# A new order of steps for the first batch of an attention and GELU kernel: squares and scalings moved between ScalarE, VectorE and GpSimd

## The chip, the cores and the metric

The kernel runs on one core of a Trainium2 chip. The metric is device time in microseconds (us), the median of several runs. Engines are named as the profile names them: PE is TensorE (PEld its weight loads), DVE VectorE, ACT ScalarE, POOL GpSimd, SP SyncE.

## What is computed

Cosine attention over 8 batches, 12 heads, 448 positions and a head size of 64, then two matrix products with an exact GELU between them, all inputs and the output in float32:

```python
q_n = q / (np.linalg.norm(q, axis=-1, keepdims=True) + 1e-06)
k_n = k / (np.linalg.norm(k, axis=-1, keepdims=True) + 1e-06)
scores = np.matmul(q_n, k_n.transpose(0, 1, 3, 2)) / tau
attn = softmax(scores, axis=-1)
x = np.matmul(attn, v)            # then to [3584, 768]
h = x @ w_in                      # w_in is [768, 2048]
g = 0.5 * h * (1.0 + erf(h / sqrt(2)))
out = g @ w_out                   # w_out is [2048, 768]
```

## The kernel before

The twelve heads of a batch are three quads of four heads. Quads are numbered through all batches, so quads 0, 1 and 2 are the first batch and quad 3 is the first of the second. A quad's q and k lie in one tile, two pairs of heads `s` side by side and the two heads of a pair on the two halves of the 128 partitions. Positions are in seven chunks `c` of 64. The normalisation works on *units*: unit 0 is pair s = 0 of quad 0, unit 1 is pair s = 1 of quad 0, and from there a unit is a whole quad (unit 2 is quad 1, unit 3 is quad 2, unit 4 is quad 3). What a unit goes through, by function and line:

- `load_qk` (L129, SP queue; the first half of k by ACT's): q and k to SBUF, in one of four buffers. `load_v` (L141), `load_wi` (L381) and `load_wo` (L388) are issued by GpSimd's queue and change the type to bf16 on the way; a `load_wi` or `load_wo` index stands for a part of the weight.
- `square(u, parts)` (L154 on ACT, L156 on GpSimd or DVE): squares of q (`Q`) or k (`K`). `reduce` (L165, DVE): their sums over the head size. `logs` (L172) and `roots` (L178 or L181), both on ACT: the root as exp(0.5 ln). `inverses` (L188 or L190, then L192): adds 1e-6 and takes the reciprocal rn, on DVE for the first batch. `scale(u, ((engine, i),))` (L208): multiplies q (i = 0) or k (i = 1) by rn into bf16; the result is the tile `qkb`.
- `transposes(u, i)` (L225, PE, seven small matmuls into a PSUM bank) and `copies(u, i)` (L230, DVE) give `qkT`. From the second batch on, a DMA transposes instead.

A quad's attention: `scores(g, ((s, c), (s, c)))` (L246, PE) gives two banks, `exps` (L253, ACT) turns both into bf16, 128x896 in one instruction; seven of these make a quad. Scores alternate between two pairs of PSUM banks, so each waits for the exps two before it. `sums` (L266) adds the rows by a matmul with ones; `turned`, `inverted` and `spread` (L297, L314, L318, DVE) make the reciprocal sums; `values` (L289, PE) multiplies with v; `normalise` (L323, DVE, one input in PSUM) writes x. A batch's x then goes through `first` (L642 `hp`, PE, and L678, the GELU on ACT) and `second_pieces` (L352 `op`, PE). `hp` of a block needs x of quads 0 and 1 first (kd 0 to 3), of quad 2 last (kd 4 and 5).

PSUM tiles for transposes and half of the values take two banks in turn. `spin(n)` (L403) issues n matmuls whose result nobody reads, into the bank that comes next in that turn; it waits for that bank to be free as the others do.

The order is set by hand: the schedule is manual, so each engine runs its instructions in the order in which the program lists them, and waits only for data and buffers. For the first batch that list is written out in `attention_first`, one call per step. For later batches `attention`, `group` and `both` set it. Before `attention_first` stand the loads, 20 spins, and `late`, a GpSimd copy that waits for the second half of the first k.

Of the kernel before, what the change touches and what calls it, by code (L numbers as in the profile page):

```python
# [16 lines left out]
def kernel(  # L17
# [129 lines left out]
    def square(u, parts=None):  # L147
        g, s0, s1 = units[u]
        if g not in sq_t:
            sq_t[g] = sqp.tile([128, 2, 2, C, D], F32, tag="sq", name=f"sq{g}")  # L150
        sq, t = sq_t[g][:, :, s0:s1], qk_t[g][:, :, s0:s1]
        for eng, part in parts or ((nc.gpsimd, slice(0, 2)),):
            if eng is nc.scalar:
                eng.activation(sq[:, part], t[:, part], AF.Square)  # L154
            else:
                eng.tensor_tensor(sq[:, part], t[:, part], t[:, part], ALU.mult)  # L156

    def reduce(u, part=slice(0, 2)):
        g, s0, s1 = units[u]
        sq = sq_t[g][:, :, s0:s1]  # L160
        n, j = place[u]
        if n not in nq_t:
            nq_t[n] = nrm.tile([128, len(groups[n]), 2, s1 - s0, C], F32, tag="nq", name=f"nq{n}")
        nq = nq_t[n][:, j]
        nc.vector.tensor_reduce(nq[:, part], sq[:, part], mybir.AxisListType.X, ALU.add)  # L165
# [239 lines left out]
    def attention_first():  # L405
        x_t[0] = xp.tile([128, KD, S], BF16, tag="x", name="x0")
        DV, AC, GP = nc.vector, nc.scalar, nc.gpsimd
        Q, K = slice(0, 1), slice(1, 2)
        square(0, ((AC, Q),))
        square(0, ((AC, K),))  # L410
        reduce(0, Q)
        reduce(0, K)
        square(1, ((AC, Q),))
        upto(load_v, 1)
        logs(0)
        reduce(1, Q)
        roots(0)
        square(1, ((AC, K),))
        inverses(0)
        square(2, ((AC, Q),))  # L420
        scale(0, ((DV, 1),))
        scale(0, ((GP, 0),))
        reduce(1, K)
        transposes(0, 1)
        upto(load_v, 2)
        transposes(0, 0)
        logs(1)
        copies(0, 1)
        roots(1)
        square(2, ((AC, K),))  # L430
        copies(0, 0)
        upto(load_wi, 1)
        inverses(1)
        spin(2)
        scores(0, ((0, 0), (0, 1)))
        square(3, ((AC, Q),))
        scores(0, ((0, 2), (0, 3)))
        reduce(2, K)
        scale(1, ((GP, 1),))
        exps(0, ((0, 0), (0, 1)))  # L440
        reduce(2, Q)
        scale(1, ((GP, 0),))
        upto(load_qk, 5)
        spin(4)
        transposes(1, 1)
        exps(0, ((0, 2), (0, 3)))
        copies(1, 1)
        logs(2)
        upto(load_wi, 2)
        spin(1)  # L450
        transposes(1, 0)
        roots(2)
        scores(0, ((0, 4), (0, 5)))
        square(3, ((AC, K),))
        inverses(2)
        copies(1, 0)
        scale(2, ((GP, 1),))
        exps(0, ((0, 4), (0, 5)))
        reduce(3, Q)
        spin(3)  # L460
        scores(0, ((1, 0), (1, 1)))
        scores(0, ((1, 2), (1, 3)))
        exps(0, ((1, 0), (1, 1)))
        reduce(3, K)
        scale(2, ((GP, 0),))
        upto(load_qk, 6)
        transposes(2, 1)
        exps(0, ((1, 2), (1, 3)))
        scores(0, ((1, 4), (1, 5)))
        copies(2, 1)  # L470
        logs(3)
        spin(1)
        scores(0, ((0, 6), (1, 6)))
        roots(3)
        upto(load_wi, 3)
        transposes(2, 0)
        exps(0, ((1, 4), (1, 5)))
        inverses(3)
        copies(2, 0)
        exps(0, ((0, 6), (1, 6)))  # L480
        scale(3, ((GP, 0),))
        spin(3)
        scores(1, ((0, 0), (1, 0)))
        exps(1, ((0, 0), (1, 0)))
        scores(1, ((0, 1), (1, 1)))
        sums(0, range(2))
        sums(0, range(2, 4))
        exps(1, ((0, 1), (1, 1)))
        scale(3, ((GP, 1),))
        scores(1, ((0, 2), (1, 2)))  # L490
        sums(0, range(4, 7))
        exps(1, ((0, 2), (1, 2)))
        scores(1, ((0, 3), (1, 3)))
        transposes(3, 0)
        turned(0)
        exps(1, ((0, 3), (1, 3)))
        upto(load_wi, 4)
        scores(1, ((0, 4), (1, 4)))
        values(0, range(2))
        copies(3, 0)  # L500
        exps(1, ((0, 4), (1, 4)))
        scores(1, ((0, 5), (1, 5)))
        inverted(0)
        transposes(3, 1)
        square(4, ((GP, K),))
        spread(0, 1)
        exps(1, ((0, 5), (1, 5)))
        scores(1, ((0, 6), (1, 6)))
        values(0, range(2, 4))
        copies(3, 1)  # L510
        values(0, range(4, 7))
        exps(1, ((0, 6), (1, 6)))
        spread(0, 0)
        square(4, ((GP, Q),))
        square(5)
        upto(load_wo, 2)
        upto(load_v, 3)
        scores(2, ((0, 0), (1, 0)))
        sums(1, range(2))
        normalise(0, 0)  # L520
        exps(2, ((0, 0), (1, 0)))
        scores(2, ((0, 1), (1, 1)))
        normalise(0, 1)
        sums(1, range(2, 4))
        exps(2, ((0, 1), (1, 1)))
        scores(2, ((0, 2), (1, 2)))
        reduce(4, K)
        sums(1, range(4, 7))
        exps(2, ((0, 2), (1, 2)))
        scores(2, ((0, 3), (1, 3)))  # L530
        values(1, range(2))
        turned(1)
        values(1, range(2, 4))
        exps(2, ((0, 3), (1, 3)))
        inverted(1)
        scores(2, ((0, 4), (1, 4)))
        spread(1, 0)
        sums(2, (0,))
        exps(2, ((0, 4), (1, 4)))
        sums(2, (1,))  # L540
        spread(1, 1)
        scores(2, ((0, 5), (1, 5)))
        values(1, range(4, 7))
        exps(2, ((0, 5), (1, 5)))
        scores(2, ((0, 6), (1, 6)))
        sums(2, (2,))
        normalise(1, 0)
        exps(2, ((0, 6), (1, 6)))
        sums(2, (3,))
        sums(2, (4,))  # L550
        reduce(4, Q)
        sums(2, (5,))
        values(2, (0,))
        sums(2, (6,))
        values(2, (1,))
        normalise(1, 1)
        logs(4)
        values(2, (2,))
        roots(4)
        values(2, (3,))  # L560
        turned(2)
        inverted(2)
        inverses(4)
        scale(4)
        spread(2, 1)
        values(2, (4,))
        values(2, (5,))
        values(2, (6,))
        spread(2, 0)
        normalise(2, 0)  # L570
        normalise(2, 1)
        done.update({square: 6, reduce: 5, root: 5, scale: 5, transposes: 5})

# [179 lines left out]
```

## Time and profile before

| what | us |
|---|---|
| median of 4 runs | 418.43 (417.96 to 418.74) |
| profiled execution | 417.54 |
| its span in the profile | 415.8 |
| PE busy | 409.4 (98%) |
| ACT busy | 246.3 (59%) |
| DVE busy | 188.1 (45%) |
| POOL busy | 167.2 (40%) |

The granted clock of TensorE is 1.00 over the span. The profile is one execution; its time is the span plus what lies around it, and it is compared with the median of the runs by the difference of the two. A row of a timeline gives the start in the span, the busy time, engine, line, operation, the tile written and those read with their shapes, the count of instructions in the row, and in brackets how long the engine sat idle before it and what ended that. Neighbouring instructions overlap by about 0.1 us in their busy times, so what an instruction costs in a full queue is the distance between starts. Matmul ends are modelled. In the first batch, ACT's first exp of quad 0 starts at 10.31, the first of quad 1 at 18.60 and the first of quad 2 at 24.56; the last ends at 30.68; the first `hp` matmul starts at 32.34.

### The profile page before, as it was taken

To read this page: it belongs to the slowest core of one execution; us is meant where nothing else is said; L and a number is where in the kernel's file an instruction comes from. 1 tells how busy PE (TensorE), PEld (TensorE's weight loads), DVE (VectorE), ACT (ScalarE), POOL (GpSimd) and SP (SyncE) were. 2 spreads that over 40 slices of the span, in tenths; PEclk is the share of its full clock that TensorE was granted. 3 is DMA by queue.
4 is the path that set the end of the run, shared out by engine and by line. 5 is a ranking of instruction groups with operands and counts; after the bars stand their busy time and mean duration, and the time that the engine had idled before them with its cause. 6 is when DMAs were issued, how large, how long until landed. Compare 5 with 4: busy or idle time off the path is not lost.

```text
span 415.8 us, 8254 instructions
## 1 busy us (share of the span) xinstructions
PE 409.4 (98%) x3506; PEld 212.3 (51%) x3506; DVE 188.1 (45%) x379; ACT 246.3 (59%) x358; POOL 167.2 (40%) x113
## 2 busy tenths in 40 slices
PE   7999999999999999999999999999999999999996
PEld 3445555555555554555555555555555554555564
DVE  5687128702676116731376314861167411661021
ACT  6995697357663578635864358734866348844300
POOL 4998615090900819063630627327270263000000
PEclk9999999999999999999999999999999999999999
DMA  8999999454563546738292372836385160430033
GB/s 293 260 259 207 202 218 258 115 93 175 102 176 75 102 164 106 174 72 233 31 233 62 73 222 52 190 75 153 114 171 145 38 90 0 85 76 2 0 77 76
DMA packets 66516, 54.53 MB, mean 131 GB/s; under 512 B 38576, under 2 KB 61488, under 8 KB 66480
## 3 DMA queue, kind: packets, MB, share of 16 engines
q1 hardware_dynamic: 53984, 41.79, 39.4%
q0 software_dynamic: 12112, 11.80, 17.8%
q8 instruction: 27, 0.44, 0.4%
q10 hardware_dynamic: 384, 0.43, 0.3%
q14 instruction: 9, 0.07, 0.1%
HBM read 45.61 MB, written 11.01 MB: 136 GB/s over the span
## 4 chain that ended last, share of the span: by engine, by line
PE 97%; DVE 1%; ACT 1%; issue 0%; DVEq 0%
PE hp L642 35%; PE op L352 35%; PE st L246 10%; PE o L289 8%; PE sm L275 4%; PE spin L403 2%; PE op L367 1%; PE sm L266 1%; PE tp L225 1%; DVE qkT L230 0%; ACT pt L253 0%; DVE rn L192 0%; DVE last L370 0%; DVE blank L85 0%; ACT root L178 0%
## 5 line engine op out<-in xcount | busy, mean ns | idle before, releaser
L253 ACT ACTIVATE pt<-st 128x896 bf16<-128x896 f32 x168 | 142.8, 916 | 39.9 <-PE st L246 38.9
L352 PE MATMUL op<-wo,g 128*128 128x384 bf16 x864 | 147.9, 327 | 0.0
L642 PE MATMUL hp<-x,wi 128*128 128x448 bf16 x768 | 146.8, 353 | 0.0
L678 ACT ACTIVATE g<-hp 128x448 bf16<-128x448 f32 x128 | 66.6, 545 | 99.5 <-PE hp L642 99.2
L352 PEld LDWEIGHTS <-g 128*128 128x128 bf16 x864 | 81.1, 98 | 63.2 <-issue 12.7
L642 PEld LDWEIGHTS <-wi 128*128 128x128 bf16 x768 | 74.5, 98 | 71.4 <-issue 2.9
L208 POOL TENSOR_TENSOR qkb<-qk,rn 128x896 bf16<-128x896 f32 (+1 forms) x49 | 79.6, 1651 | 46.3 <-DVE rn L192 46.3
L165 DVE TENSOR_REDUCE nq<-sq 128x28 f32<-128x1792 f32 (+2 forms) x30 | 48.7, 1634 | 64.0 <-POOL sq L156 61.3
L156 POOL TENSOR_TENSOR sq<-qk 128x1792 f32<-128x1792 f32 (+1 forms) x22 | 66.8, 3040 | 13.1 <-DMA qk<-in_k_dram 13.0
L356 DVE COPY ot<-op 128x384 f32<-128x384 f32 x54 | 29.5, 546 | 69.6 <-PE op L352 69.6
L190 POOL TENSOR_SCALAR se<-sr 128x28 f32<-128x28 f32 (+1 forms) x14 | 4.4, 311 | 122.6 <-ACT sr L181 122.5
L246 PE MATMUL st<-qkT 64*64 64x448 bf16 x672 | 48.3, 359 | 0.3
L289 PE MATMUL o<-pt,v 64*64 64x448 bf16 x672 | 36.9, 352 | 0.0
L246 PEld LDWEIGHTS <-qkT 64*64 64x64 bf16 x672 | 18.2, 105 | 25.6 <-issue 18.1
L192 DVE RECIPROCAL rn<-se 128x28 f32<-128x28 f32 (+2 forms) x18 | 6.8, 377 | 51.3 <-POOL se L190 51.1
L318 DVE STREAM_TRANSPOSE rs<-rc 128x448 f32<-128x448 f32 x48 | 28.1, 623 | 0.8
L297 DVE STREAM_TRANSPOSE tr<-sm 128x448 f32<-128x448 f32 x24 | 15.6, 650 | 28.5 <-PE sm L275 25.4
L323 DVE TENSOR_TENSOR x<-o,rs 128x448 bf16<-128x448 f32 x48 | 27.0, 600 | 1.0 <-DVE rs L318 0.5
L289 PEld LDWEIGHTS <-v 64*64 64x64 bf16 x672 | 17.7, 106 | 15.8 <-issue 7.2
L275 PE MATMUL sm<-pt,ones 128*32 128x448 bf16 (+1 forms) x336 | 19.3, 332 | 0.0
L309 DVE TENSOR_REDUCE tr<-tr 32x28 f32<-32x28 f32 x84 | 16.5, 197 | 1.6
L275 PEld LDWEIGHTS <-ones 128*32 128x32 bf16 x336 | 7.4, 95 | 10.6 <-issue 8.9
(43 smaller groups left out, 118.3 us busy)
## 6 DMA issues: line engine op xcount, KB each, us to landing
out_dram<-ot SPq DMA_DIRECT2D x54, 192.0 KB, 2.8
qk<-in_q_dram SPq DMA_DIRECT2D x23, 448.0 KB, 5.6
qk<-in_k_dram SPq DMA_DIRECT2D x23, 448.0 KB, 6.5
v<-in_v_dram POOLq DMA_DIRECT2D x7, 672.0 KB, 10.8
wi<-in_moe_w_in_dram POOLq DMA_DIRECT2D x8, 384.0 KB, 14.1
wo<-in_moe_w_out_dram POOLq DMA_DIRECT2D x4, 768.0 KB, 14.1
qk<-in_q_dram SPq DMA_DIRECT2D x2, 224.0 KB, 3.4
v<-in_v_dram POOLq DMA_DIRECT2D x1, 448.0 KB, 7.7
```

Source lines behind the costliest of these rows:

```text
L156: eng.tensor_tensor(sq[:, part], t[:, part], t[:, part], ALU.mult)
L165: nc.vector.tensor_reduce(nq[:, part], sq[:, part], mybir.AxisListType.X, ALU.add)
L208: eng.tensor_tensor(qkb[:, i, :, s0:s1].rearrange("p c s d -> p s c d"), t[:, i, s0:s1], rn[:, i].to_broadcast([128, s1 - s0, C, D]), ALU. ...
L246: nc.tensor.matmul(st[cols, n, :S], lhsT=qkT[rows, 1, c, cols], rhs=qkT[rows, 0, :, cols], start=True, stop=True, tile_position=(64 * s, 6 ...
L253: nc.scalar.activation(pt[:, :m], st[:, :m, :S], AF.Exp, scale=inv_tau)
L275: nc.tensor.matmul(bank_t[g, "sm"][r:r + 32, cols], lhsT=ones, rhs=pt_t[g, s, c][:, cols], start=(c < 2), stop=(c >= C - 2), tile_position ...
L289: nc.tensor.matmul(bank_t[g, h][cols, :S], lhsT=v_t[g][rows, s, c, :], rhs=pt_t[g, s, c][rows], start=(c == 0), stop=(c == C - 1), tile_po ...
L318: nc.vector.transpose(rs, bank_t[g, "rc"][:, h].to_broadcast([128, NB, 32]))
L352: nc.tensor.matmul(ps[:, :NH], lhsT=g_t[sb][:, kf, t * 128:(t + 1) * 128], rhs=wo[:, kf, ni * NH:(ni + 1) * NH], start=(kf == 0), stop=(kf ...
L356: nc.vector.tensor_copy(ot[:, ni * NH:(ni + 1) * NH], ps[:, :NH])
L642: nc.tensor.matmul(hps[m], lhsT=wi[:, kd, m * 128:(m + 1) * 128], rhs=x_t[b][:, kd, :], start=(kd == 0), stop=(kd == KD - 1))
L678: nc.scalar.activation(g_t[sb][:, m, hf * S:(hf + 1) * S], hps.pop(m), AF.Gelu)
```

## The change

Only the list in `attention_first` changes; each instruction is there before and after, apart from the spins, of which two fewer stand in the list (12 instead of 14). What moves from one engine to another:

| step | before | after |
|---|---|---|
| square of unit 0, q (128x448) | ACT | DVE |
| square of unit 1, k (128x448) | ACT | GpSimd |
| square of unit 3, k (128x896) | ACT | GpSimd |
| scale of unit 0, k (128x448) | DVE | GpSimd |
| scale of unit 2, k (128x896) | GpSimd | DVE |
| scale of unit 3, k (128x896) | GpSimd | DVE |

And the order: the squares of quad 1 on ACT stand behind the roots of units 0 and 1, those of q of quad 2 in front of the first exps; the reduces of quad 2 stand earlier on DVE; loads of w_in stand later among GpSimd's steps; one square of quad 3 stands in front of the scaling of quad 2. The tail of quad 2 is reordered a little. The diff, with unchanged stretches left out:

```diff
-        square(0, ((AC, Q),))
+        square(0, ((DV, Q),))
         square(0, ((AC, K),))
         reduce(0, Q)
+        square(1, ((AC, Q),))
         reduce(0, K)
-        square(1, ((AC, Q),))
         upto(load_v, 1)
+        reduce(1, Q)
         logs(0)
-        reduce(1, Q)
         roots(0)
-        square(1, ((AC, K),))
+        square(1, ((GP, K),))
         inverses(0)
-        square(2, ((AC, Q),))
-        scale(0, ((DV, 1),))
         scale(0, ((GP, 0),))
         reduce(1, K)
+        logs(1)
+        scale(0, ((GP, 1),))
+        spin(1)
+        transposes(0, 0)
+        roots(1)
+        square(2, ((AC, Q),))
+        square(2, ((AC, K),))
+        upto(load_v, 2)
+        inverses(1)
+        spin(1)
         transposes(0, 1)
-        upto(load_v, 2)
-        transposes(0, 0)
-        logs(1)
+        copies(0, 0)
+        square(3, ((AC, Q),))
         copies(0, 1)
-        roots(1)
-        square(2, ((AC, K),))
-        copies(0, 0)
-        upto(load_wi, 1)
-        inverses(1)
+        reduce(2, Q)
         spin(2)
         scores(0, ((0, 0), (0, 1)))
-        square(3, ((AC, Q),))
-        scores(0, ((0, 2), (0, 3)))
         reduce(2, K)
         scale(1, ((GP, 1),))
+        scores(0, ((0, 2), (0, 3)))
         exps(0, ((0, 0), (0, 1)))
-        reduce(2, Q)
         scale(1, ((GP, 0),))
         upto(load_qk, 5)
-        spin(4)
+        spin(1)
         transposes(1, 1)
+        reduce(3, Q)
         exps(0, ((0, 2), (0, 3)))
+        scores(0, ((0, 4), (0, 5)))
+        upto(load_wi, 1)
+        square(3, ((GP, K),))
+        transposes(1, 0)
         copies(1, 1)
         logs(2)
-        upto(load_wi, 2)
-        spin(1)
-        transposes(1, 0)
         roots(2)
-        scores(0, ((0, 4), (0, 5)))
-        square(3, ((AC, K),))
+        copies(1, 0)
+        exps(0, ((0, 4), (0, 5)))
         inverses(2)
-        copies(1, 0)
-        scale(2, ((GP, 1),))
-        exps(0, ((0, 4), (0, 5)))
-        reduce(3, Q)
-        spin(3)
+        spin(2)
         scores(0, ((1, 0), (1, 1)))
         scores(0, ((1, 2), (1, 3)))
-        exps(0, ((1, 0), (1, 1)))
-        reduce(3, K)
+        scale(2, ((DV, 1),))
         scale(2, ((GP, 0),))
         upto(load_qk, 6)
+        exps(0, ((1, 0), (1, 1)))
+        exps(0, ((1, 2), (1, 3)))
+        spin(3)
+        scores(0, ((1, 4), (1, 5)))
+        reduce(3, K)
         transposes(2, 1)
-        exps(0, ((1, 2), (1, 3)))
-        scores(0, ((1, 4), (1, 5)))
+        upto(load_wi, 2)
+        exps(0, ((1, 4), (1, 5)))
+        scores(0, ((0, 6), (1, 6)))
+        transposes(2, 0)
         copies(2, 1)
+        square(4, ((GP, Q),))
+        exps(0, ((0, 6), (1, 6)))
+        copies(2, 0)
         logs(3)
-        spin(1)
-        scores(0, ((0, 6), (1, 6)))
+        spin(2)
+        scores(1, ((0, 0), (1, 0)))
+        sums(0, range(2))
         roots(3)
+        exps(1, ((0, 0), (1, 0)))
         upto(load_wi, 3)
-        transposes(2, 0)
-        exps(0, ((1, 4), (1, 5)))
         inverses(3)
-        copies(2, 0)
-        exps(0, ((0, 6), (1, 6)))
-        scale(3, ((GP, 0),))
-        spin(3)
-        scores(1, ((0, 0), (1, 0)))
-        exps(1, ((0, 0), (1, 0)))
         scores(1, ((0, 1), (1, 1)))
-        sums(0, range(2))
         sums(0, range(2, 4))
+        scale(3, ((DV, 1),))
         exps(1, ((0, 1), (1, 1)))
-        scale(3, ((GP, 1),))
         scores(1, ((0, 2), (1, 2)))
         sums(0, range(4, 7))
+        scale(3, ((GP, 0),))
         exps(1, ((0, 2), (1, 2)))
         scores(1, ((0, 3), (1, 3)))
-        transposes(3, 0)
+        transposes(3, 1)
         turned(0)
         exps(1, ((0, 3), (1, 3)))
+        scores(1, ((0, 4), (1, 4)))
+        copies(3, 1)
+        values(0, range(2))
         upto(load_wi, 4)
-        scores(1, ((0, 4), (1, 4)))
-        values(0, range(2))
-        copies(3, 0)
+        inverted(0)
         exps(1, ((0, 4), (1, 4)))
         scores(1, ((0, 5), (1, 5)))
-        inverted(0)
-        transposes(3, 1)
-        square(4, ((GP, K),))
+        transposes(3, 0)
         spread(0, 1)
         exps(1, ((0, 5), (1, 5)))
         scores(1, ((0, 6), (1, 6)))
+        spread(0, 0)
         values(0, range(2, 4))
-        copies(3, 1)
-        values(0, range(4, 7))
-        exps(1, ((0, 6), (1, 6)))
-        spread(0, 0)
-        square(4, ((GP, Q),))
+        square(4, ((GP, K),))
         square(5)
         upto(load_wo, 2)
         upto(load_v, 3)
+        copies(3, 0)
+        values(0, range(4, 7))
+        exps(1, ((0, 6), (1, 6)))
+        reduce(4, Q)
         scores(2, ((0, 0), (1, 0)))
+        scores(2, ((0, 1), (1, 1)))
         sums(1, range(2))
+        exps(2, ((0, 0), (1, 0)))
         normalise(0, 0)
-        exps(2, ((0, 0), (1, 0)))
-        scores(2, ((0, 1), (1, 1)))
-        normalise(0, 1)
         sums(1, range(2, 4))
         exps(2, ((0, 1), (1, 1)))
         scores(2, ((0, 2), (1, 2)))
-        reduce(4, K)
+        normalise(0, 1)
         sums(1, range(4, 7))
...
         inverted(1)
         scores(2, ((0, 4), (1, 4)))
-        spread(1, 0)
+        spread(1, 1)
         sums(2, (0,))
         exps(2, ((0, 4), (1, 4)))
-        sums(2, (1,))
-        spread(1, 1)
         scores(2, ((0, 5), (1, 5)))
+        spread(1, 0)
         values(1, range(4, 7))
         exps(2, ((0, 5), (1, 5)))
         scores(2, ((0, 6), (1, 6)))
+        sums(2, (1,))
+        normalise(1, 0)
         sums(2, (2,))
-        normalise(1, 0)
         exps(2, ((0, 6), (1, 6)))
         sums(2, (3,))
+        normalise(1, 1)
+        values(2, (0,))
+        values(2, (1,))
+        reduce(4, K)
         sums(2, (4,))
-        reduce(4, Q)
         sums(2, (5,))
-        values(2, (0,))
         sums(2, (6,))
-        values(2, (1,))
-        normalise(1, 1)
         logs(4)
-        values(2, (2,))
+        turned(2)
         roots(4)
-        values(2, (3,))
-        turned(2)
         inverted(2)
+        spread(2, 0)
         inverses(4)
         scale(4)
-        spread(2, 1)
+        values(2, (2,))
+        values(2, (3,))
         values(2, (4,))
         values(2, (5,))
         values(2, (6,))
-        spread(2, 0)
         normalise(2, 0)
+        spread(2, 1)
         normalise(2, 1)
```

## The prediction

> **What bounds the kernel now.** I read the chain of waits first, then the busy time by stage, then the timelines of the engines over the first 33 us. The chain's shares by engine and by line:
>
> ```profile
> PE 97%; DVE 1%; ACT 1%; issue 0%; DVEq 0%
> PE hp L642 35%; PE op L352 35%; PE st L246 10%; PE o L289 8%; PE sm L275 4%; PE spin L403 2%; PE op L367 1%; PE sm L266 1%; PE tp L225 1%; DVE qkT L230 0%; ACT pt L253 0%; DVE rn L192 0%; DVE last L370 0%; DVE blank L85 0%; ACT root L178 0%
> ```
>
> The chain is TensorE almost throughout, and the stages show where another engine has a say (columns: length, then busy time and count of PE, PEld, DVE, ACT, POOL, granted clock, DMA share, GB/s):
>
> ```profile
> 4.08:10.31 6.23, 5.95 (x39) 3.15 (x37) 5.11 (x12) 5.48 (x12) 4.37 (x6) 1.00 1.04 376
> 10.31:18.60 8.29, 7.85 (x72) 3.61 (x68) 7.19 (x12) 7.74 (x14) 8.25 (x10) 1.00 1.16 261
> 18.60:24.56 5.96, 5.96 (x86) 3.06 (x87) 3.38 (x7) 5.88 (x8) 5.94 (x6) 1.00 1.11 260
> 24.56:32.34 7.78, 7.78 (x109) 3.09 (x107) 6.93 (x12) 7.14 (x10) 7.44 (x6) 1.00 1.11 252
> ...
> 45.00:410.00 365.00, 365.00 (x3107) 189.76 (x3105) 155.86 (x316) 210.83 (x305) 129.96 (x75) 1.00 0.52 117
> ```
>
> From 32.34 us, the first hp matmul, PE never rests: whatever the first batch gains or loses shifts the end one for one. From 10.31 to 18.6 DVE, ACT and POOL are 87%, 93% and 99% busy, and to 24.56 ACT and POOL stay at 99%, so a step moved from one to another lands on a full engine. TensorE, from its timeline:
>
> ```profile
> 23.20 1.12 PE L289 MATMUL o<-pt,v 64*64 64x448 bf16 x20
> 24.15 0.36 PE L246 MATMUL st<-qkT 64*64 64x448 bf16 x4
> ...
> 31.08 1.33 PE L289 MATMUL o<-pt,v 64*64 64x448 bf16 x24
> 32.34 1.88 PE L642 MATMUL hp<-x,wi 128*128 128x448 bf16 x9
> ```
>
> 24.15 is scores(2,0), the start of quad 2; from there to hp are 8.19 us of gapless PE work. GpSimd:
>
> ```profile
> 5.50 0.94 POOL L141 DMA_DIRECT2D v<-in_v_dram  x1
> 7.00 1.36 POOL L208 TENSOR_TENSOR qkb<-qk,rn 128x448 bf16<-128x448 f32 x1 [0.57 <-DVE rn L192]
> ...
> 10.39 1.85 POOL L208 TENSOR_TENSOR qkb<-qk,rn 128x448 bf16<-128x448 f32 x2
> 12.17 1.29 POOL L381 DMA_DIRECT2D wi<-in_moe_w_in_dram  x2
> 13.48 3.34 POOL L208 TENSOR_TENSOR qkb<-qk,rn 128x896 bf16<-128x896 f32 x2
> ```
>
> A 128x448 product takes 0.93, a 128x896 one 1.65 to 1.69, a pair of wi issues 1.29. But the first one took 1.36, beside the only DVE product with both inputs in SBUF:
>
> ```profile
> 6.94 0.63 DVE L208 TENSOR_TENSOR qkb<-qk,rn 128x448 bf16<-128x448 f32 x1
> 7.49 0.61 DVE L165 TENSOR_REDUCE nq<-sq 128x7 f32<-128x448 f32 x1
> ...
> 9.93 2.01 DVE L165 TENSOR_REDUCE nq<-sq 128x14 f32<-128x896 f32 x2
> ```
>
> ACT: a 448 square costs 0.47 start to start, an 896 one 0.84, an exp 0.81.
>
> **The change, part by part.** The queues are strict lists, so I carry start times through them with those rows; a handover costs 0.03 to 0.09.
>
> *First scores.* square(0,Q) on DVE (0.63, as the 448 product) ends at 4.71, reduce(0,Q) and (0,K) follow at 4.74 and 5.27, logs(0) runs at 5.92 (now 5.87) and rn of unit 0 is there at 6.96 (now 6.91): +0.05. Then GpSimd has in series what two engines did side by side: the v issue (to 6.43), square(1,K) to 7.37, scale(0,0) to 8.28, scale(0,1) to 9.20. Today both scales are done by 8.36. The last transposes start 0.06 to 0.22 behind (both occur), take 0.56, the copy 0.63: copies(0,1) ends at 10.47 to 10.63 and the first scores start at 10.55 to 10.7, now 9.71. The first exp, 0.61 behind, starts at 11.15 to 11.3, now 10.31. ACT idles from 6.48 until logs(1) at 8.10 (square(1,K) 7.37, reduce 0.61), then runs the squares of quad 1 and Q of quad 2 to 11.1. inverses(1) now stands before both copies on DVE, but ends at 9.13, before the one that counts can start: nothing.
>
> *Second half of quad 0.* ACT has no square(3,K) here, saving 0.84: exps(0,4) starts at 13.3 to 13.4, now 13.56. DVE takes it back: three reduces of 128x896 (2,Q; 2,K; 3,Q), 3.0 us in all, stand before copies(1,·), where two do now. Copies(1,0) ends 4.05 behind copies(0,1), at 14.5 to 14.7 (now 14.05), so exps(0,(1,0)) starts at 15.2 to 15.35, now 14.73, and ACT waits 1.0 for it.
>
> *Quad 1.* rn of unit 2 follows copies(1,0) by 0.6: 15.1 to 15.3. DVE's scale(2,1) (0.63 plus the 0.46 by which a reduce grows from 448 to 896: 1.09) and GpSimd's scale(2,0) start together. Alone, the latter ends 1.78 after rn, at 16.9 to 17.05 (now 16.82 with both on GpSimd). Beside a DVE product the 7.00 row lost 0.43 of its time against 0.63 of DVE's, so I take 0.7 for 1.09; the bounds are 0 (no gain: the products without such a neighbour all take 1.69) and 1.09, since a product on DVE cannot block GpSimd longer than it runs. With 0.7: 17.6 to 17.75, and copies(2,0), with scores(1,0) behind it, is 0.2 later than without.
>
> *Quad 2, the step that decides.* On GpSimd follow wi(1) 1.29, square(4,Q) 1.65, wi(2) 1.29, scale(3,0) 1.69: 5.9 us, today scale(3,0) and (3,1) come straight after one wi pair and end at 21.42. DVE's scale(3,1), at 19.65, falls on square(4,Q): 0.7 again. scale(3,0) ends at 24.2 to 24.35. Behind transposes(3,0), which waits for it on PE, stand scores(1,6), the values of quad 0 and scores(2,0). By the PE rows (transposes 0.50, scores 0.21, twenty values 0.95, handover 0.06) scores(2,0) starts 1.72 after scale(3,0): 25.9 to 26.1, against 24.15: +1.75 to +1.95. Without any stall scale(3,0) ends at 22.8 to 22.95, PE's own list (5.97 us from scores(1,0) at 18.7 to 18.85) is as late, and scores(2,0) starts at 24.65 to 24.8: +0.5 to +0.65.
>
> The 7.00 row has one witness. The Trainium skill ("GPSIMD Engine Reference", Key points) says that GpSimd shares its SBUF interfaces with VectorE and contends with its instructions that have two SBUF inputs; it speaks against scale(2,1) and scale(3,1) on DVE and gives no price. The trace has the other side too: the normalise products (L323, one input in PSUM) run at 24.39 beside GpSimd squares that keep 1.69.
>
> *Tail.* From scores(2,0) to hp the same matmuls run with scores(2,1) directly behind scores(2,0) and two switches fewer between kinds of matmul on the way: block by block 7.95 instead of 8.19, with exps about equally quick: -0.2. Moving reduce(4,·), logs(4), turned and spread costs nothing: hp of kd 0 to 3 covers them for 3.8 us, and they are no later relative to sums(2,6).
>
> *DMAs.* The wi pairs are issued at about 11.8, 17.6, 22, 24.3 (now 9.13, 12.17, 16.76, 21.35). They land today near 21, 27, 32 and 36, one per 5 us, so the queue sets this, and each is still issued before the one ahead lands; hp needs the second at 34. wo and v go out some 1.5 later; wo lands near 43 now and is first read at 52, v near 48 and 60. If that cover failed, it would cost the lateness itself. Two spins fewer cost nothing while PE waits anyway.
>
> *Sum.* +1.85 at scores(2,0), -0.2 in the tail: +1.65. The profiled execution took 417.54 (span 415.76 and 1.78 around it), so 419.2; the median of the runs is 0.89 above it, 418.43: **420.1 us**.
>
> **Rivals.** A measurement of this kernel tells no less than about 0.2%, 0.84 us, from no change.
>
> *No stall on GpSimd.* The DVE products cost it nothing: +0.55 - 0.2, 418.8. For it: GpSimd is unmoved by all other DVE work. Against: the 7.00 row.
>
> *The 1.36 is a first use*, the first product of the run, and not the neighbour. Then square(1,K) pays 0.43, and everything to scores(1,0) is that much later, with no stall later on: +0.8, 419.2. The trace can't separate these two, since that product was both.
>
> *Faster: ACT's release carries through.* ACT loses two 448 squares and one 896, 1.78 us. If scores(1,0) started by 17.5 (PE's list from there to hp is 0.2 shorter; now 18.16), the gain would pass 0.84; all of it would give 416.7. It needs copies(0,1) done by about 9.3, so GpSimd's three products in about half their 0.93 each. No row does that; hence little chance.
>
> *A cold TensorE.* The first spins go out every 0.37 until 5.62 and every 0.19 from then. Between 7.6 and 10.7 PE would have about 1.3 us without work, against 1.0 today. Falling back to 0.37 for some 3 us would double up to 2 us of work around the first scores: +0.35 and 2, 420.8, and 421 or more with a stall as well. The Trainium skill ("TensorE: Matmul & The Clock Gate", Part 1) puts the fall behind an idle window of about 3.4 us, which no gap here reaches; no run so far shows a fall.
>
> **How the numbers follow.** Stall as in the row: 0.48. No stall: 0.21. First use: 0.13, half over the bound. Faster: 0.10. Cold: 0.08. Slower 0.48 + 0.07 + 0.08 = 0.63, within 0.2% 0.21 + 0.06 = 0.27, faster 0.10. The likeliest case alone spans 419.2 (half the stall) to 420.9 (1.09 each). The range must reach the unstalled case with some play, 418.2, and the cold one, 421.2; what is left out is nearly only the faster case.
>
> **What would show it.** Right: first exp near 11.2; exps(0,(1,0)) near 15.3 with 1 us of ACT waiting; scale(2,0) and square(4,Q) on GpSimd at about 2.4 instead of 1.69; PE waiting on GpSimd's qkb before transposes(3,0) near 24.3; hp near 34. Wrong: those two products at 1.69 (no stall), square(1,K) at 1.36 (first use), hp before 32.3 (ACT's release), matmuls 0.37 apart after 8 us (cold).

## The result and the profile after

The changed kernel takes **419.25 us** (median of 46 runs, 418.97 to 420.63) against **418.13 us** for the kernel before (71 runs, 417.50 to 421.03). The ratio is 1.0027, with a 95% interval of 1.0022 to 1.0032: slower by 1.13 us, between 0.92 and 1.34. The prediction was 420.1 us in a range of 418.2 to 421.2, with 0.63 on slower.

The profiled execution of the changed kernel took 419.69 us. Its chain of waits, by engine and by line, is the counterpart of the first fence of the prediction:

```profile
PE 93%; POOL 4%; issue 2%; DVE 0%; POOLq 0%
PE hp L643 35%; PE op L352 35%; PE st L246 9%; PE o L289 8%; PE sm L275 4%; POOL qkb L208 1%; PE op L367 1%; POOL sq L156 1%; POOL wi L381 1%; PE sm L266 1%; POOL v L141 0%; PE tp L225 0%; POOL ident masks.py:199 0%; DVE last L370 0%; POOL ident masks.py:197 0%
```

"PE spin L403 2%" is gone from it, and GpSimd's products, squares and wi issues have come in. The chain that ends last now starts on another engine.

That execution isn't on equal footing with the profile of before: `late`, which waits for the second half of the first k, starts at 5.97 in it and at 5.37 in before. A second profile of the same changed kernel (experiment 1; 419.06 us, span 417.3) has `late` at 5.37 too, and the readings below are of that one. Its stages, cut at the same events as in the prediction (first exp of quad 0, of quad 1, of quad 2, first `hp`; columns as there):

```profile
4.08:11.15 7.07, 6.35 (x41) 3.00 (x39) 5.51 (x12) 4.60 (x10) 5.74 (x8) 1.00 1.06 365
11.15:19.71 8.56, 7.05 (x66) 3.31 (x64) 7.81 (x13) 6.72 (x12) 7.95 (x8) 1.00 1.15 269
19.71:26.23 6.52, 6.14 (x88) 2.77 (x86) 6.35 (x9) 5.99 (x7) 6.48 (x7) 1.00 1.10 270
26.23:33.89 7.66, 7.66 (x108) 3.20 (x105) 6.73 (x12) 6.75 (x10) 6.71 (x6) 1.00 1.12 226
```

Against before, the head is 0.84 longer (11.15 for 10.31), quad 0's stage 0.27 (8.56 for 8.29), quad 1's 0.56 (6.52 for 5.96), and the last is 0.12 shorter (7.66 for 7.78). The sum is +1.55 at `hp`, and the two executions are 1.52 apart. In quad 0's stage PE now rests for 1.51 us (8.56 less 7.05; before 0.44) and in quad 1's for 0.38 (before none). ACT, 93% busy in quad 0's stage before, is 79% busy now (6.72 of 8.56): it was relieved and then waits. In quad 1's stage DVE has gone from 3.38 of 5.96 to 6.35 of 6.52. The chain of waits of this profile, in order of time (start, length, what):

```profile
5.37 0.18 POOL late L698
5.55 0.88 POOL v L141
6.43 0.02 issue
6.46 0.95 POOL sq L156
7.41 1.78 POOL qkb L208 x2
9.19 0.76 POOL v L141
...
11.80 1.25 POOL wi L381 x2
13.06 0.01 issue
13.07 1.70 POOL sq L156
...
22.13 1.93 POOL qkb L208
24.06 0.05 issue
24.11 0.56 PE tp L225 x7
```

Up to 24.06 the chain is GpSimd's list, started by the landing of k; the product that ends there is scale(3,0), and PE takes over with transposes(3,0) 0.05 later. It has one break, in the stretch between the wi issues at 11.80 and the product at 22.13: before scale(2,0), at 15.35, GpSimd stands idle for 0.58 until DVE has rn, so up to there DVE's list has its say too. GpSimd's timeline shows what the neighbour on DVE does to it, and DVE's shows the reverse:

```profile
6.46 0.95 POOL L156 TENSOR_TENSOR sq<-qk 128x448 f32<-128x448 f32 x1
7.35 1.84 POOL L208 TENSOR_TENSOR qkb<-qk,rn 128x448 bf16<-128x448 f32 x2
...
15.35 2.59 POOL L208 TENSOR_TENSOR qkb<-qk,rn 128x896 bf16<-128x896 f32 x1 [0.58 <-DVE rn L192]
17.89 1.29 POOL L381 DMA_DIRECT2D wi<-in_moe_w_in_dram  x2
19.20 1.69 POOL L156 TENSOR_TENSOR sq<-qk 128x896 f32<-128x896 f32 x1
20.82 1.29 POOL L381 DMA_DIRECT2D wi<-in_moe_w_in_dram  x2
22.13 1.92 POOL L208 TENSOR_TENSOR qkb<-qk,rn 128x896 bf16<-128x896 f32 x1
```

```profile
15.30 1.09 DVE L208 TENSOR_TENSOR qkb<-qk,rn 128x896 bf16<-128x896 f32 x1
...
18.60 0.62 DVE L230 COPY qkT<-tp 128x896 bf16<-128x896 bf16 x1 [0.55 <-PE tp L225]
...
19.76 2.74 DVE L208 TENSOR_TENSOR qkb<-qk,rn 128x896 bf16<-128x896 f32 x1
```

At 15.30 DVE's scale(2,1) starts 0.05 ahead of GpSimd's scale(2,0): DVE keeps its 1.09, and GpSimd takes 2.59 instead of 1.69. At 19.20 GpSimd's square(4,Q) is 0.56 ahead of DVE's scale(3,1): GpSimd keeps 1.69, and DVE takes 2.74 instead of 1.09.

### The profile page after: what moved, and what is told of

Its sections match the earlier page's. It is cut to its first block, busy times and chain, and to the rows that moved or that the text cites. A ratio compares the mean times of both kernels' runs of the same rounds, so it can differ in the third digit from the quotient of the medians.

```text
span 417.9 us, 8250 instructions
## 1 busy us (share of the span) xinstructions
PE 409.7 (98%) x3504; PEld 211.8 (51%) x3504; DVE 191.9 (46%) x381; ACT 244.5 (59%) x355; POOL 168.2 (40%) x114
## 3 DMA queue, kind: packets, MB, share of 16 engines
q0 software_dynamic: 12112, 11.80, 18.0%
## 4 chain that ended last, share of the span: by engine, by line
PE 93%; POOL 4%; issue 2%; DVE 0%; POOLq 0%
PE hp L643 35%; PE op L352 35%; PE st L246 9%; PE o L289 8%; PE sm L275 4%; POOL qkb L208 1%; PE op L367 1%; POOL sq L156 1%; POOL wi L381 1%; PE sm L266 1%; POOL v L141 0%; PE tp L225 0%; POOL ident masks.py:199 0%; DVE last L370 0%; POOL ident masks.py:197 0%
## 5 line engine op out<-in xcount | busy, mean ns | idle before, releaser
L208 POOL TENSOR_TENSOR qkb<-qk,rn 128x896 bf16<-128x896 f32 (+1 forms) x48 | 78.0, 1650 | 46.5 <-DVE rn L192 46.5
L156 POOL TENSOR_TENSOR sq<-qk 128x1792 f32<-128x1792 f32 (+2 forms) x24 | 69.5, 2899 | 10.3 <-DMA qk<-in_k_dram 10.1
L246 PEld LDWEIGHTS <-qkT 64*64 64x64 bf16 x672 | 18.1, 105 | 26.3 <-issue 17.6
L289 PEld LDWEIGHTS <-v 64*64 64x64 bf16 x672 | 17.6, 106 | 15.8 <-issue 7.3
```

The lines of the kernel that those rows point to most:

```text
L208: eng.tensor_tensor(qkb[:, i, :, s0:s1].rearrange("p c s d -> p s c d"), t[:, i, s0:s1], rn[:, i].to_broadcast([128, s1 - s0, C, D]), ALU. ...
L246: nc.tensor.matmul(st[cols, n, :S], lhsT=qkT[rows, 1, c, cols], rhs=qkT[rows, 0, :, cols], start=True, stop=True, tile_position=(64 * s, 6 ...
L289: nc.tensor.matmul(bank_t[g, h][cols, :S], lhsT=v_t[g][rows, s, c, :], rhs=pt_t[g, s, c][rows], start=(c == 0), stop=(c == C - 1), tile_po ...
```

## The experiments

Starts, as in the prediction, are us in each kernel's own profile. Each timed kernel is given with the kernel before as run on the same chip. The ratio and its interval are taken over the runs of both, so they aren't the quotient of the two medians.

**1. The changed kernel again**, nothing edited, to part the landing of k from the list.

> The changed kernel once more, for a second profile beside the edits of it. In the first profile the second half of k of quad 0 landed at 5.97 us (late, on GpSimd), in the profile of before at 5.37, and everything on GpSimd follows it. Theory A (chance of one execution): late starts near 5.4 here, scores(2,0) near 25.8 and hp near 33.9, the span is about 417.4 and the median stays at 419.2. Theory B (the new list itself delays that landing, since DVE or GpSimd start differently): late starts near 6.0 again, hp near 34.5, the same median.

419.41 us against 418.12, ratio 1.0025 (1.0010 to 1.0041). Between the two profiles of this kernel `late` is 0.60 apart, `hp` 0.61 (34.50 and 33.89) and the time 0.63. In the new list a late landing of k goes through to the end one for one, and at equal landing the change costs 1.52.

**2. GpSimd's square behind the product.** In the changed kernel, square(4,Q) goes from before scale(3,0) to after it:

```diff
         copies(2, 1)
-        square(4, ((GP, Q),))
...
         scale(3, ((GP, 0),))
+        square(4, ((GP, Q),))
```

> The changed kernel with one step moved: q of quad 3 is squared on GpSimd behind scale(3,0), not in front of it. Theory A (GpSimd's list sets scores(2,0)): scale(3,0) ends about 1.5 sooner, then PE's own list from scores(1,0) is last, scores(2,0) starts 0.5 sooner: about 418.7. Theory B (the meeting of products on DVE and GpSimd is the cost, wherever it falls): scale(3,1) now meets scale(3,0) instead of the square, no gain: 419.2. Theory C (the late first scores are the whole loss): no gain either, 419.2, with transposes(3,0) no longer waiting.

419.21 us against 418.12, ratio 1.0024 (1.0007 to 1.0040). GpSimd's rows, then DVE's:

```profile
17.96 2.53 POOL L381 DMA_DIRECT2D wi<-in_moe_w_in_dram  x4
20.50 1.98 POOL L208 TENSOR_TENSOR qkb<-qk,rn 128x896 bf16<-128x896 f32 x1
```

```profile
19.84 1.09 DVE L208 TENSOR_TENSOR qkb<-qk,rn 128x896 bf16<-128x896 f32 x1
```

Now DVE's scale(3,1) is the first to start (19.84) and takes 1.09, with wi issues of GpSimd beside it until 20.49; scale(3,0), from 20.50, takes 1.98 and ends at 22.48 instead of 24.05. Transposes(3,0) wait for it no more, and from scores(1,0) to scores(2,0) it is 6.17 us instead of 6.52. So square(4,Q)'s place, with DVE's stall, is worth 0.35 in quad 1; the medians differ by 0.2, which they don't settle. PE's own order of this quad takes 0.18 more than the 5.99 of before even so.

**3. Both halves on GpSimd.** In the changed kernel, so that no product of DVE with two SBUF inputs lies beside GpSimd:

```diff
-        scale(2, ((DV, 1),))
+        scale(2, ((GP, 1),))
...
-        scale(3, ((DV, 1),))
+        scale(3, ((GP, 1),))
```

> The changed kernel with scale(2,1) and scale(3,1) back on GpSimd, at the same places in the list. Theory A (GpSimd's list): two products of 1.65 more, less the 0.9 and 0.2 that the meetings cost: scale(3,0) ends 2.2 later, hp 2.2 later, about 421.4. Theory B (the meetings with DVE's products are the whole cost): the loss goes, about 418.1. In both, no product on GpSimd takes over 1.7 for 896.

421.93 us against 418.12, ratio 1.0092 (1.0060 to 1.0124). The pairs run for 3.33 and 3.34, 1.69 an instruction, and `hp` starts at 36.65. This profile has `late` at 6.04, so 0.67 of the 2.76 by which `hp` is behind experiment 1 is landing, and about 2.1 the GpSimd work. DVE's help, with a stall of 0.90 on GpSimd and of 1.65 on DVE, is still the cheaper choice in this list: the stalls are part of what the change costs, but the products have to run somewhere.

**4. The head of before under the new list.** In the changed kernel, square(0,Q) and square(1,K) go back to ACT, scale(0,1) to DVE, and quad 0's transposes and copies to the order that goes with it:

```diff
-        square(0, ((DV, Q),))
+        square(0, ((AC, Q),))
...
-        square(1, ((GP, K),))
+        square(1, ((AC, K),))
         inverses(0)
+        scale(0, ((DV, 1),))
         scale(0, ((GP, 0),))
...
-        scale(0, ((GP, 1),))
```

> The changed kernel with the assignments of before for units 0 and 1: q of unit 0 and k of unit 1 squared on ACT, k of unit 0 scaled on DVE. Theory A (GpSimd's three products in series at the start delay the scores, and the delay is carried to the end): first scores near 9.75, copies(1,0), rn of unit 2, scale(2,0) and scale(3,0) all some 0.9 sooner: about 418.3. Theory B (ACT gets to its first exp at 11.1 in either list, so the head costs nothing): 419.2. Theory C (DVE's three reduces before copies(1,0) are the loss): they start 0.9 sooner too, but wait for ACT's squares, ready at 9.5, 10.4 and 11.2: copies(1,0) gains 0.9 only if DVE is never idle between them, else about 0.6: 418.6.

419.56 us against 418.12, ratio 1.0034 (1.0016 to 1.0051): nothing gained, where the head's 0.84 was expected back. The execution that was profiled (421.39) can't tell why. In it the loads of quads 1 and 2 landed late: ACT's three squares of 128x896 waited 0.52, 0.25 and 0.22 for them, and the first exp started at 12.45. And TensorE's granted clock fell; the window from 16 to 18 us (the clock is the number after POOL's):

```profile
16.00:18.00 2.00, 2.00 (x9) 0.47 (x7) 1.86 (x2) 1.52 (x2) 2.00 (x1) 0.50 1.13 282
```

**5. That kernel again**, for a profile that can be read.

> The changed kernel with the head of before, profiled once more: in the first profile TensorE's granted clock was 0.5 from 15.4 to 22.2 us, so that its steps can't be read. Theory A (the head's 0.95 is carried to the end): exps(0,(1,0)) near 14.4, scores(2,0) near 25.0, time about 418.3. Theory B (the squares that this list puts in front of the first exps hold ACT until 11.1, and GpSimd's list from there on is the one that counts): first exp at 11.1 or later, exps(0,(1,0)) near 14.4 to 15.3, scores(2,0) within 0.3 of the changed kernel's 25.8, time about 419.2.

418.77 us, one execution, clock 1.00. First scores at 9.94 instead of 10.54, yet the first exp at 11.24 instead of 11.15. ACT's timeline:

```profile
8.72 2.61 ACT L154 ACTIVATE sq<-qk 128x896 f32<-128x896 f32 x3
11.24 1.70 ACT L253 ACTIVATE pt<-st 128x896 bf16<-128x896 f32 x2
...
15.04 3.35 ACT L253 ACTIVATE pt<-st 128x896 bf16<-128x896 f32 x4 [0.83 <-PE st L246]
```

Three squares of 128x896 stand before the first exp, and they end at 11.33 whatever the scores do. DVE's three reduces run from 10.17 to 13.18 on those squares, with copies(1,·) behind them. Scores(2,0) start at 25.51 instead of 25.80 and `hp` at 33.60 instead of 33.89: the head's delay is worth 0.3 of the 1.55, not 0.84. The first q landed 0.13 later in this profile (ACT's first square starts at 4.21, at 4.08 in before), so at equal landing I estimate 0.4. The median of experiment 4 doesn't show even that, and why is open; loads that land late, as in its profile, are a candidate. This profile also has GpSimd's first product beside DVE's again: 1.36, from 7.13, against DVE's 0.62 from 7.08, while experiment 1, without DVE's product there, has the two at 1.84 together.

**6. The kernel before again**, nothing edited.

> The kernel before, profiled once more; its times lie in two heaps, near 417.7 and near 418.4, and the profile shown so far (417.54) is of the lower one. Theory A (loads of quads 1 and 2 land later in about half of the executions and hold ACT's squares): if the time is near 418.4, ACT waits for q or k by 0.3 or more in front of a square, and scores(2,0) starts later than 24.15 by as much as hp does; if it is near 417.7 there is no such wait. Theory B (the heaps come from behind hp): hp starts at 32.3 in either case.

417.91 us, 0.37 above the first profile; `hp` at 32.72 instead of 32.34. PE's timeline, first of the profile of before, then of this execution:

```profile
1.93 5.83 PE L403 MATMUL spin<-blank,ident 128*128 128x448 bf16 x20 [1.93 <-DVE root L89]
7.81 1.18 PE L225 MATMUL tp<-ident,qkb 128*64 128x128 bf16 x14
```

```profile
1.93 6.30 PE L403 MATMUL spin<-blank,ident 128*128 128x448 bf16 x20 [1.93 <-DVE root L89]
8.29 0.94 PE L225 MATMUL tp<-ident,qkb 128*64 128x128 bf16 x14
```

No transfer is late here. The spins go from 0.37 apart to 0.19 apart at 6.74 instead of 5.62, so the twenty end 0.47 later, and transposes(0,1), whose product DVE ended at 7.56, stand behind them. I read the turn as a rise of TensorE's clock. 0.37 apart is also the pace of spins where experiment 4 has the granted clock at 0.50 (starts at 16.74 and 17.12), and the record of the clock in these two traces begins at full rate at 5.79 and 6.75; that it holds nothing before is why a window says 1.00 on both sides of the turn. Neither theory had named this. The chain of before had begun with "PE spin L403" all along. Two other profiles with all but this head fit: with the turn at 4.87 (experiment 11) `hp` starts at 32.35, with the turn at 6.74 (experiment 7) at 32.78. In the changed kernel the turn came at 6.73 in its first profile and cost nothing there: its first transposes waited 0.33, until 8.96, for GpSimd's scale(0,0). But k had landed late in that execution. The spins before those transposes ended at 8.63, and in experiment 1 (turn at 5.24) the transposes start at 8.35; a late turn with an early k, which no profile of the changed kernel has, could hold them by up to 0.28.

**7. The fourth load held back in before.** A GpSimd memset after scale(0,0) makes the load of quad 3 go out later, as a test of whether it delays the loads of quads 1 and 2:

```diff
         qk_t[g] = t
+        if g == 3:
+            nc.gpsimd.memset(t[:, 0, 0, 0, 0:1], 0.0)
...
         scale(0, ((GP, 0),))
+        upto(load_qk, 4)
...
-    upto(load_qk, 4)
```

> The kernel before, with the load of quad 3 (not needed before 22 us) held back until GpSimd has done scale(0,0), by a memset of one element of its tile there (0.1 us on GpSimd). Theory A (loads in flight together delay those of quads 1 and 2 in some executions): the upper heap goes, median about 417.7. Theory B (the heaps have another cause): unchanged, 418.1.

418.31 us against 418.04, ratio 0.9996 (0.9974 to 1.0019): no difference. The runs still lie between 417.87 and 420.46, so the spread of before doesn't come from that load.

**8. Three spins fewer in before**, to free its first transposes from a late rise of the clock:

```diff
-    spin(20)
+    spin(17)
```

> The kernel before with 17 opening spins in place of 20. In its first profile the spins turn from 0.37 to 0.19 apart at 5.62 and the first transposes start at 7.81; in the second the turn comes at 6.74, the spins run to 8.2 and the transposes start at 8.29, hp 0.38 later. Theory A (before is held by its opening spins when TensorE's clock rises late, the changed kernel is not, because GpSimd feeds its first transposes at 8.35 anyway; this is why the medians differ by less than the profiles): three spins less free 0.6 to 1.1, the low end of the times stays at 417.5 to 417.7, the median falls by 0.2 to 0.4 to about 417.8. Theory B (the spread of before has another cause): same median, 418.1. Theory C (fewer spins leave TensorE at the slow rate more often): median above 418.5, matmuls 0.37 apart behind 8 us.

417.93 us against 418.17, ratio 0.9991 (0.9970 to 1.0012). With the rise at 6.36 the first transposes start at 7.65. The sign fits, and no faster median was measured, but the interval holds no change as well.

**9. The new tail in before.** From scores(2,0) on, before gets the order of the changed list, with one slip: reduce(4,Q) stands in front of normalise(0,1), where the change has nothing.

> The kernel before, with only the new order of the steps from scores(2,0) on (q's reduce of quad 3 left where k's stood). Theory A (two switches fewer on a full TensorE): scores(2,0) to hp takes 8.0 to 8.1 instead of 8.19, the median 0.1 to 0.2 lower, 418.0. Theory B (the exps set the tail): no change, 418.1.

418.93 us against 418.04, ratio 1.0011 (0.9993 to 1.0029). In its profile the reduce waits 1.02 us for GpSimd's square, normalise(0,1) stands behind it on DVE, and PE's values of quad 1 wait 0.35 for that:

```profile
29.61 0.95 PE L289 MATMUL o<-pt,v 64*64 64x448 bf16 x15 [0.35 <-DVE x L323]
```

From scores(2,0) to `hp` it is 8.98 us instead of 8.19. This says what one misplaced step costs, and nothing of the tail.

**10. The same with the slip mended**: k's reduce, whose square is done in time, behind normalise(0,1).

```diff
-        reduce(4, Q)
         normalise(0, 1)
+        reduce(4, K)
...
-        reduce(4, K)
+        reduce(4, Q)
```

> The kernel before with the new order from scores(2,0) on, and the two reduces of quad 3 in the order in which GpSimd squares them there, k first and behind normalise(0,1). In the first try q's reduce stood in front of normalise(0,1) on DVE and waited 1.0 for GpSimd's square, and the values of quad 1 waited for that normalise; scores(2,0) to hp took 8.98. Theory A (two switches fewer): 8.0 to 8.1 from scores(2,0) to hp, median 418.0. Theory B (no change): 8.2, 418.1.

418.15 us against 418.17, ratio 0.9992 (0.9977 to 1.0007). From scores(2,0) to `hp` it is 8.27 us. The new order of the tail is worth nothing on before, and 0.1 in the changed kernel (8.09).

**11. Every later pair of products split between DVE and GpSimd in before**, to see many such pairs:

```diff
-        for eng, i in parts or ((nc.gpsimd, 0), (nc.gpsimd, 1)):
+        for eng, i in parts or ((nc.vector, 1), (nc.gpsimd, 0)):
```

> The kernel before, with k of every quad from the second batch on (and of quad 3) scaled on DVE and only q on GpSimd, to measure by itself what a DVE product with both inputs in SBUF and a GpSimd product cost each other. Theory A (whichever starts first keeps the way to SBUF, the other stands still meanwhile): where DVE starts first it takes 1.09 and GpSimd 2.4 to 2.6; where GpSimd starts first it takes 1.69 and DVE's product ends about 1.1 after GpSimd's does. Theory B (GpSimd always yields): DVE 1.09 always, GpSimd 2.4 to 2.6 always. Theory C (the 1.36 of the first product and the 2.60 were something else): 1.09 and 1.69 throughout. The time may go either way by a microsecond or two and decides nothing.

420.9 us, one execution, `hp` unchanged at 32.35. The groups of its products, by form:

```profile
L208 POOL TENSOR_TENSOR qkb<-qk,rn 128x896 bf16<-128x896 f32 x25 | 54.1, 2177 | 45.7 <-DVE rn L192 45.7
L208 DVE TENSOR_TENSOR qkb<-qk,rn 128x896 bf16<-128x896 f32 x21 | 39.1, 1887 | 0.3
```

GpSimd's mean is 2177 ns where it was 1688 in before, and DVE's 1887 where 1.09 us is its time undisturbed. The means mix two cases. First a pair that DVE starts (GpSimd's row, then DVE's), then one that GpSimd starts, with the square that follows:

```profile
32.85 2.59 POOL L208 TENSOR_TENSOR qkb<-qk,rn 128x896 bf16<-128x896 f32 x1 [0.74 <-DVE rn L192]
...
103.65 1.69 POOL L208 TENSOR_TENSOR qkb<-qk,rn 128x896 bf16<-128x896 f32 x1 [0.44 <-DVE rn L192]
105.30 4.02 POOL L156 TENSOR_TENSOR sq<-qk 128x1792 f32<-128x1792 f32 x1
```

```profile
32.80 1.09 DVE L208 TENSOR_TENSOR qkb<-qk,rn 128x896 bf16<-128x896 f32 x1
...
103.89 2.39 DVE L208 TENSOR_TENSOR qkb<-qk,rn 128x896 bf16<-128x896 f32 x1
```

DVE ahead by 0.05: 1.09 and 2.59. GpSimd ahead by 0.24: 1.69 and 2.39, and then GpSimd's next square takes 4.02 where its group in before has 3.17 (63.5 us by 20), because DVE's waiting product goes first. The one ahead isn't slowed at all; the other stands still.

**12. One reduce later.** In the changed kernel, reduce(3,Q) goes from before copies(1,·) to just before reduce(3,K):

```diff
         transposes(1, 1)
-        reduce(3, Q)
...
+        reduce(3, Q)
         reduce(3, K)
```

> The changed kernel with DVE's reduce of q of quad 2 moved from in front of copies(1,·) to behind scale(2,1), in front of the reduce of k. Theory A (DVE is full from 10.4 to 19.2, so an order of its steps only moves the wait): exps(0,(1,0)) starts near 14.7 instead of 15.3 and rn of unit 2 near 14.6, but copies(2,0) ends near 19.1 as before, since the reduce now stands in front of it; quad 1 starts at 19.7 as now, the time is 419.2 to 419.4. Theory B (the third reduce in front of the copies is the loss of quad 0): all from exps(0,(1,0)) on is 0.6 sooner, time about 418.7.

419.06 us against 418.25, ratio 1.0021 (1.0012 to 1.0030). Exps(0,(1,0)) start at 14.83, 0.49 sooner, and scale(2,0) at 14.85. But on DVE the reduce now stands before copies(2,·):

```profile
15.81 2.07 DVE L165 TENSOR_REDUCE nq<-sq 128x14 f32<-128x896 f32 x2
17.91 1.16 DVE L230 COPY qkT<-tp 128x896 bf16<-128x896 bf16 x2
```

Copies(2,0) end at 19.07 instead of 19.22: of 0.49 gained, 0.15 is left (k landed 0.11 later here, so both gains are some 0.1 larger at equal landing). DVE is full between 10 and 19 us, and a step that moves takes its wait along. What the stall of scale(2,0) is worth this doesn't tell: the stall is there as before (2.59 from 14.85), and DVE has no idle time left in front of copies(2,0). A bound stands in DVE's row at 18.60 of experiment 1: DVE is idle for 0.55 before copies(2,0), and without the stall no more than that could come back there.

## Why the prediction was right, and where it was not

**The head and the landing of quad 1: right.** At equal landing the first scores start at 10.54 (10.55 to 10.7 foreseen), the first exp at 11.15 (11.15 to 11.3), exps(0,4) at 13.24 (13.3 to 13.4); copies(1,0) end at 14.66 (14.5 to 14.7), and exps(0,(1,0)) start at 15.32 (15.2 to 15.35) after ACT has waited 1.19 for them (1.0). GpSimd's queue in series sets the first scores, DVE's third reduce sets exps(0,(1,0)), as argued. What the prediction didn't see is that the first of these matters little: experiment 5 took most of the head's delay away and got 0.3 to 0.4 back.

**scale(2,0): mechanism right, size short.** 2.59 instead of the 2.4 taken, so a stall of 0.90 instead of 0.7, within the bounds of 0 and 1.09. It ends at 17.94 (17.6 to 17.75), and scores(1,0), 1.34 behind it in both kernels, start at 19.28: +1.12. The product's own end is 0.90 later by the stall and 0.22 by the later start. Without the stall at most 0.55 of the 0.90 would come back (experiment 12), because DVE's copies then come last.

**square(4,Q): wrong engine.** The step "falls on square(4,Q): 0.7 again" failed. square(4,Q) kept 1.69 and scale(3,1) took 2.74. The one witness, the row at 7.00, had DVE 0.06 ahead, and the prediction read it as GpSimd being the one that yields; experiments 1, 2 and 11 show that the later starter yields, whichever engine it is. The Trainium skill ("SBUF — State Buffer", Who interferes with whom) says that a DVE instruction with two SBUF inputs contends with a GpSimd one that reads SBUF, and that the order of issue decides who blocks; that the first keeps the shared ports for its whole instruction it says of DVE's 2-port modes, which a product of two tensors doesn't have. The runs agree for the first starter in each pair. For the second, losing the whole overlap would be 0.14 too much: scale(2,0) overlaps DVE's product by 1.04 and lost 0.90, scale(3,0) of experiment 2 overlaps by 0.43 and lost 0.29, DVE's product at 103.89 of experiment 11 overlaps by 1.45 and lost 1.30. Only scale(3,1) lost more than its overlap: 1.65, at 1.13 beside the square.

**scale(3,0) and scores(2,0): right, through errors of opposite sign, so with luck.** scale(2,0) 0.2 to 0.35 later, square(4,Q) 0.7 shorter, and scale(3,0) itself 1.92 since DVE's late product still ran until 22.50 beside it: the end is 24.05 (24.2 to 24.35). Scores(2,0) start at 25.80, +1.65 where +1.75 to +1.95 was foreseen. Of quad 1's +0.53 from scores to scores, experiment 2 gives 0.35 back. So of the +1.55 at `hp` the runs account for the head's 0.3 to 0.4, that 0.35, PE's own order with 0.18 and the tail with -0.10. Some 0.7 to 0.8 is left, all of it before scores(1,0); the stall of scale(2,0) and DVE's third reduce lie there, and no run parts them.

**The tail: sign right, size short.** -0.10 (8.09 for 8.19) where -0.2 was foreseen. Sum at `hp`: +1.55 against +1.65, and 419.06 for the execution against 419.2.

**The term that was mis-sized is the last one: from the profile to the median.** The prediction added 0.89, the gap between the profile of before and the median of its four runs. Over 71 runs that gap is 0.59, and for the changed kernel it is 0.19 (419.25 less 419.06). Carried over, it made 0.70 of the 0.85 by which 420.1 was too high. The profile of before, at 417.54, was near the lowest of its runs (417.50). TensorE's clock rose early in it; with a late rise the first transposes wait behind the spins (+0.37 in experiment 6). The changed kernel's runs begin closer to their median (418.97 and 419.25); that it is less open to a late rise is argued from its first transposes, which wait for GpSimd, and isn't shown. So the medians are 1.12 apart where the lowest runs are 1.47 and the two executions 1.52 apart. The page of before held the hint: "PE spin L403 2%" in its chain. That the clock's rise makes up the whole of the gap isn't shown; late landings and a fall of the clock are the other candidates. One sum of the prediction is off, without weight: with half the stall, 0.35 each, its own terms give about 419.4 and not 419.2.

**The rivals.** *No stall* fell with 2.59 and 2.74. *First use* fell with square(1,K), GpSimd's first product in the changed kernel: 0.95, with 1.84 for the two after it. *ACT's release* fell with ACT's idle time, 1.63 before logs(1) and 1.19 before exps(0,(1,0)): the squares that it lost came back as waits for GpSimd and DVE. *A cold TensorE*: in the profile of experiment 1 the granted clock is 1.00 in every stage, and after 8 us spins still go out close together (two in 0.55 us from 9.76). A fall was seen in one profile of experiment 4, with a list that differs in its head; so it can happen. It isn't what the change costs: over the whole span the clock is 0.991 in that profile, and in none of the changed kernel's 46 runs is it below 0.998.

None of the kernels of the experiments beats before by more than the runs can tell; experiment 8's 417.93 comes closest.

## What to carry to other kernels

When a step is moved to relieve a full engine, carry the lists of all the others through to the next place where two of them meet: here ACT gave up 1.78 us of squares and got them back as idle time, because GpSimd and DVE, which took them, fed the very steps that ACT waits for. Before products with two SBUF inputs are split between DVE and GpSimd, ask which of the two starts first, and let that be the one whose result is wanted first; the time of the other is its own work and nearly the whole overlap. And before the gap between one profile and the median is carried over to a changed kernel, look at what the head of the chain hangs on: a gap that comes from one kernel's own first wait isn't the other's.

## What the runs showed of the hardware

- **Who stands still.** For 128x896 products beside each other: the one that starts first keeps its time (DVE 1.09, GpSimd 1.69), the other stands still for the overlap less some 0.14, which makes up to 2.59 on GpSimd and 2.39 or 2.58 on DVE (experiment 11). The next point has the exception. DVE's other work, reduces and copies among it, left GpSimd's 1.69 alone.
- **More than the wait.** scale(3,1) ran from 19.76 to 22.50; GpSimd's square had ended at 20.89, and 1.61 remained for a product of 1.09. Two wi issues of GpSimd lie beside that rest (20.82 to 22.11). In experiment 12, with the issues behind the square as well, 1.87 remained; in experiment 11, with GpSimd's product ahead and no issue behind, 0.94. Issues beside a product that is already running did nothing: scale(3,1) of experiment 2 kept 1.09 with issues beside it. Whether they hold up one that waits wasn't tried by itself, and what set the rest is open.
- **The turn of the opening spins wanders.** With the first matmul at 1.93 in each, the turn from 0.37 to 0.19 per spin came at 5.62 and 6.74 in two executions of before, at 5.24 and 6.73 in two of the changed kernel, and at 4.50 in experiment 5. A list whose first useful matmul stands behind the spins wanders with it (`hp` at 32.34 and 32.72 in before).
- **The clock can fall without a long pause.** In experiment 4's profile it was 0.50 for 6.8 us from about 15.7 us on; no idle time of PE between the first spin and there was longer than 1.22 us, though PE was busy for only 0.78 of the 2 us from 12 to 14. The Trainium skill ("TensorE: Matmul & The Clock Gate", Part 1) puts a fall behind an idle window of about 3.4 us, but also tells of a kernel whose frequent short pauses made the clock go to and fro; this fall came without the long pause, and what set it off is open.
